# Four chunks to a cycle: a new order of score, V-product and dense matmuls in an attention and GEGLU block on one core

## The chip, the cores and the metric

The kernel runs on one core of one Trainium2 chip. The metric is the device time of one execution in microseconds: 1398.37 us, the median of 3 runs (1397.21 to 1399.72).

## The reference

A transformer block in fp32 on 2048 rows of 512: attention with 32 heads of 16 columns that share one k and one v, then a GEGLU with 1792 inner columns.

```python
h = x + A(layernorm(x), wq, wk, wv, wo)
    # q = x @ wq in 32 heads; k = x @ wk; v = x @ wv
    # softmax(q k^T * 16**-0.5) v, then @ wo
h2 = h + (gelu(xn @ w_gate) * (xn @ w_up)) @ w_down      # xn = layernorm(h)
```

## The kernel before

**Attention.** The scores are computed transposed, keys on partitions. The 2048 queries are four blocks b of 512, the 32 heads are eight groups g of four, the 2048 keys are 16 pieces kc of 128. One index i runs over all 4 x 8 x 16 = 512 of these; one i is called a *chunk* here. For a chunk, `scores` (L361 to L374) issues two *score pairs* u = 0, 1: two matmuls of 50 rows on the two halves of TensorE's array, for two heads, into a tile s of two PSUM banks, and then one exp on ScalarE (ACT) from s into half of the chunk's tile p. The tile s has two buffers (a third one in the first quarter of the run, L361 to L365), p has five (PB). `weigh` (L376 to L381) then multiplies the four heads' p with v: four matmuls on four column groups of the array, into one accumulator bank acc for the 16 chunks of a group; behind the 16th, `evacuate` copies acc to oT on VectorE (L391) and sends it by DMA to be turned and divided. Chunks that are scored and not yet weighed stand in the list `pend`; `finish(n)` weighs the n oldest.

**Dense work.** For the first three query blocks the output projection, the GEGLU's up and down products (`project`, `up`, `down`, matmul on L797) run between the attention matmuls of later blocks. Every product is split in two halves by rows of the contraction: `firsts` issues the first half (rows 0 to 63) of one product, and `seconds`, six matmuls later (LAG), the second half (rows 64 to 127) of it; the two lie side by side on the array. `step()` issues one matmul of each, and is called a *half step* here. Each half product ends in a bank of its own, out of three, that VectorE must copy or add out (L660, L664, L727) before the bank is used again; with it, `side(2)` issues up to two more VectorE operations of the GELU that are waiting in `later`. The tanh is on ACT (L676). `turn` (L623) transposes a normalized tile of h. The last block's dense work is the tail (`last_dense`, L899 and L835), after all attention.

**The order.** Nothing is scheduled by a planner: TensorE, ACT and POOL, and in this part VectorE and SP, take the order in which the code is written. After the prologue and a first quarter without dense work (`PERIOD`), a loop of `lead` scores fills the pipeline, and then the loop under L1134 runs to the end of the attention. It goes through `CYCLES`, three strings in turn: `finish(count)` at a cycle's start, then one letter a move: s a score pair, d a half step, v `finish(1)`. Three cycles take 3 + 3 + 2 chunks, 16 score pairs and 11 + 11 + 14 half steps. If there are not enough half steps available for the string (dense products wait for the normalization and the turns of a block), the cycle is *idle*: what half steps there are go first, and the second string, with single v's and no d's, is used.

Of the kernel before, what the change touches and what calls it, by code (L numbers as in the profile page):

```python
# [43 lines left out]

SETTLE = 14

CYCLES = (
    (3, "ssdddddsdddsddds", "vssvssvs"),
    (3, "ssdddddsdddsddds", "vssvssvs"),
    (2, "ssdddddsdddsdddsddds", "ssvssvss"),  # L50
)

BOUND_LISTS = (3, 4)

HOLD = -4

# [3 lines left out]
def kernel(  # L60
# [97 lines left out]
    def run(outer, first):  # L158
# [400 lines left out]
        tanhs, later = [], []  # L559
        clock = 0  # L560
# [117 lines left out]
        def gate(b, f):  # L678
            g, u, a = (halves.pop((b, f, k)) for k in range(3))

            def bring():
                nc.vector.scalar_tensor_tensor(a, a, 1.0, g, op0=ALU.add, op1=ALU.mult)

            def weigh_up():
                nc.vector.tensor_tensor(a, a, u, op=ALU.mult)

            def high():
                key = b, f // 2
                if key not in gs:
# [12 lines left out]

            return [bring, weigh_up, high, low]
# [103 lines left out]
        def step(first=True):  # L807
            nonlocal ahead, clock
            clock += 1
            if first and next(firsts, 0) is None:  # L810
                ahead += 1
            if ahead > LAG or not first:
                assert ahead > 0
                next(seconds)
                ahead -= 1
# [35 lines left out]
        last_x = []  # L851

        def prepare_x():
            b = NB - 1
            xp = sb.tile([P, TB, D], F32, tag="p", bufs=PB, name=f"xp_{b}")
            for t in range(TB):
                nc.gpsimd.dma_start(xp[:, t, :], x_t[:, b * TB + t, :])
                last_x.append(xp[:, t, :])
# [137 lines left out]
        PER = NG * KC  # L996
# [5 lines left out]
        def finish(n):  # L1002
            for _ in range(min(n, len(pend))):
                pb, pg, pkc, pp, pacc, _ = pend.pop(0)
                weigh(pacc, pp, pkc)
                if pkc == KC - 1:
                    evacuate(pb, pg, pacc)
# [9 lines left out]
        def score(n):  # L1017

            nonlocal acc
            i, u = divmod(n, 2)  # L1020
            b, r = divmod(i, PER)
            g, kc = divmod(r, KC)
            if u == 0:
                if kc == 0:
                    cur["qg"] = qgs.pop((b, g))
                    acc = psa.tile([P, T], F32, tag="acc", bufs=1, name=f"acc_{b}_{g}")
                if kc == 2 and b * NG + g + 1 < NB * NG:
                    key = divmod(b * NG + g + 1, NG)
                    qgs[key] = load_q(*key)
                cur["p"] = sb.tile([P, 4, T], F32, tag="p", bufs=PB, name=f"p_{i}")  # L1030
            scores(i, cur["p"], cur["qg"], kc, u)
            if u == 1:
                pend.append((b, g, kc, cur["p"], acc, n))
# [9 lines left out]
        width = 1  # L1043


        n, lead = 0, 2 * PER + 23
        with tc.manual_schedule(engines={mybir.EngineType.SP, mybir.EngineType.DVE}):
            parts = None
            if first:
                work = later_q()  # L1050
                parts = part_weights(early.enter_context(tc.tile_pool(name="parts", bufs=1)))


            normed = True

            def visit():
                nonlocal work, normed
                total, k = 0, None
                while work is not None and total < 6 and k != 2:
                    k = next(work, None)  # L1060
                    if k is None:
                        work = None
                        return
                    total += k
                normed = k != 4

            def norm():
                nonlocal normed
                if not normed:
                    next(work)  # L1070
                    normed = True

            def pace():
                nonlocal n, parts, db, tiny
                if n == 2 * PER:
                    drain()
                    for _ in parts or ():
                        pass
# [12 lines left out]
                if n == 2 * PER + 8:  # L1091
                    prime()

            moves = {"s": pace, "p": visit, "n": norm, "v": partial(finish, 1)}
            for move in OPENING + PERIOD * (PER // KC):
                moves[move]()
            while n < lead:
                pace()
                if n % 4 == 2 and len(pend) > 2 and n < lead - 1:
                    finish(1)  # L1100
                elif n % 4 == 0:
                    finish(len(pend) - 2)
# [5 lines left out]
        def catch_up():  # L1108
            while ahead > 0:
                step(False)  # L1110

        def before(idle):
            if outs:
                take_out()
            while (b_t := divmod(sum(turned.values()), TB)) in scaled_at:
                if clock - scaled_at[b_t] < SETTLE:
                    break
                turn(*b_t)
                if not idle:
                    break  # L1120
            bent = list(tanhs)
            tanhs.clear()
            for key in bent:
                bend(*key)
            side(100 if idle else 2)
            return bent
# [5 lines left out]
        fixed.enter_context(  # L1132
            tc.manual_schedule(engines={mybir.EngineType.SP, mybir.EngineType.DVE})
        )  # L1134
        for i in range(-((lead - end) // 16)):
            if first and i in BOUND_LISTS:
                bound_flag(BOUND_LISTS.index(i))
            for count, woven, plain in CYCLES:
                idle = available() < woven.count("d")
                if idle:  # L1140
                    while available():
                        step()
                    if at == len(queue) or queue[at][0].startswith("pg"):
                        catch_up()
                bent = before(idle)
                if n == end and not last_x:
                    prepare_x()
                if not idle:
                    finish(count)
                for key in bent:  # L1150
                    later.extend(gate(*key))
                for move in plain if idle else woven:
                    if move == "d":
                        step()
                    elif move == "v":
                        if n == end and not last_x:
                            prepare_x()
                        finish(1)
                        clock += 4
                    elif n < end:  # L1160
                        score(n)
                        n += 1
                        clock += 1
        fixed.close()
        assert not pend and not outs and at == len(queue) and left[0] == 0
        held_banks.close()
# [307 lines left out]
    def bound_flag(step):  # L1474
        if step == 0:
            nc.gpsimd.dma_start(b2, b_d)
            return
        nc.vector.tensor_reduce(b1, b2, axis=AX.X, op=ALU.max)

        nc.vector.tensor_scalar(flag, b1, (BOUND_MAX / SCALE) ** 2, None, op0=ALU.is_le)  # L1480
# [69 lines left out]
```

## Time and profile before

| | |
|---|---|
| median of 3 runs | 1398.37 us |
| the profiled execution, its own time | 1399.75 us |
| its span in the profile | 1398.0 us |
| TensorE busy | 1384.1 us, 99% |
| ACT busy | 1033.8 us, 74% |
| VectorE busy | 630.1 us, 45% |
| mean TensorE clock granted | 0.998 |

The profile names an engine's instructions by line of the kernel: PE is TensorE, PEld its weight loads, DVE VectorE. A row of the timeline has its start and its length in us, engine, line, operation, out<-in, the shape (rows x columns of the array in use, then what is read), how many like it stand in a row, and in brackets how long the engine had been idle and what ended that. A row of a group has busy time, the mean of one in ns, and the idle time before. The scores are L370, their exps L374, the V-products L378; the program's four V-products of a chunk stand in the trace as eight.

### The profile page before, as it was taken

Reading aid. Unit: us, or ns where it says so; the run is one execution under the profiler, and the core shown is the slowest. Engines: PE = TensorE matmul, PEld = TensorE weight load, DVE = VectorE, ACT = ScalarE, POOL = GpSimd, SP = SyncE. Lnnn points to the kernel's source line nnn. Section 1 sums busy time; section 2 is a strip of 40 time slices with the busy share of each in tenths; the row PEclk is TensorE's granted clock in tenths of the full one; section 3 lists DMA queues with packets and bytes.
Section 4 is the critical chain, followed back from the end, with each engine's and each line's share of the span. In section 5 each row is a group of like instructions: output and inputs, shape, how many; then the busy total and the mean of one; then the engine's idle time right before and its main releaser. Section 6 shows DMA issues by size and latency. Waiting matters only on the chain.

```text
span 1398.0 us, 25236 instructions
## 1 busy us (share of the span) xinstructions
PE 1384.1 (99%) x10430; PEld 754.1 (54%) x10430; DVE 630.1 (45%) x1013; ACT 1033.8 (74%) x1157; POOL 229.5 (16%) x334
## 2 busy tenths in 40 slices
PE   9999999999999999999999999999999999999998
PEld 7533333325555555545555555545555555558886
DVE  7413131314354444555354444446264453546665
ACT  8899999997787777877787777787778777772000
POOL 7576777721000000000000000000000000011000
PEclk9999999999999999999999999999999999999999
DMA  4466777753232332311432433320433333233552
GB/s 163 167 207 195 233 245 221 229 183 117 79 103 76 118 103 103 112 64 58 162 100 80 134 103 103 103 65 29 150 103 103 114 107 100 93 122 123 190 204 95
DMA packets 66783, 180.32 MB, mean 129 GB/s; under 512 B 9672, under 2 KB 9672, under 8 KB 66628
## 3 DMA queue, kind: packets, MB, share of 16 engines
q1 hardware_dynamic: 55324, 143.29, 31.1%
q0 software_dynamic: 10208, 35.26, 7.7%
q8 instruction: 84, 1.38, 0.4%
q14 instruction: 39, 0.32, 0.1%
q10 hardware_dynamic: 1128, 0.07, 0.1%
HBM read 130.87 MB, written 47.45 MB: 128 GB/s over the span
## 4 chain that ended last, share of the span: by engine, by line
PE 95%; ACT 2%; DVE 1%; issue 1%; DMA 1%; POOL 0%; ACTq 0%; POOLq 0%
PE acc L378 33%; PE s L370 20%; PE pu L797 9%; PE pg L797 8%; PE pd L797 7%; PE pq L219 3%; PE pd L835 3%; PE pg L835 3%; PE pu L835 3%; PE pp L797 2%; ACT p L374 2%; PE pp L899 1%; PE pd_rest L847 1%; PE pk L1295 1%; PE idle L1355 1%
## 5 line engine op out<-in xcount | busy, mean ns | idle before, releaser
L374 ACT ACTIVATE p<-s 128x1024 f32<-128x1024 f32 x1024 | 959.3, 1038 | 226.3 <-PE s L370 223.4
L378 PE MATMUL acc<-p,v_sb 128*32 128x512 f32 x4096 | 491.2, 599 | 0.0
L370 PE MATMUL s<-qg,kaug 50*128 50x512 f32 x1984 | 386.0, 427 | 4.2 <-ACT p L374 4.1
L370 PEld LDWEIGHTS s<-qg,kaug 50*128 50x128 f32 x1984 | 168.8, 184 | 282.9 <-ACT p L374 123.5
L378 PEld LDWEIGHTS acc<-p,v_sb 128*32 128x32 f32 x4096 | 108.8, 109 | 233.3 <-issue 219.9
L797 PE MATMUL pg<-x2h,w 64*128 64x512 f32 x672 | 174.8, 392 | 0.0
L797 PE MATMUL pu<-x2h,w 64*128 64x512 f32 x672 | 174.2, 392 | 0.0
L797 PE MATMUL pd<-w,gh 64*128 64x512 f32 x624 | 123.1, 394 | 0.3
L727 DVE TENSOR_TENSOR h<-h,pd 128x512 f32<-128x512 f32 x80 | 54.9, 687 | 146.0 <-PE pd L797 146.0
L137 POOL TENSOR_SCALAR rstd<-mv 128x1 f32<-128x1 f32 x16 | 3.6, 223 | 674.2 <-DVE mv L135 673.9
L797 PEld LDWEIGHTS pu<-x2h,w 64*128 64x128 f32 x672 | 95.4, 186 | 11.5
L797 PEld LDWEIGHTS pg<-x2h,w 64*128 64x128 f32 x672 | 95.1, 186 | 11.7
L797 PE MATMUL pg<-x2l,w 64*128 64x512 f32 x336 | 99.9, 392 | 0.0
L797 PE MATMUL pu<-x2l,w 64*128 64x512 f32 x336 | 99.9, 392 | 0.0
L953 ACT ACTIVATE ga<-ga 128x512 f32<-128x512 f32 x14 | 8.8, 632 | 88.5 <-DVE ga L950 88.5
L797 PEld LDWEIGHTS pd<-w,gh 64*128 64x128 f32 x624 | 67.6, 185 | 12.3 <-DVE u L664 1.4
L391 DVE COPY oT<-acc 128x512 f32<-128x512 f32 x32 | 22.1, 691 | 113.4 <-PE acc L378 113.3
L797 PE MATMUL pd<-w,gl 64*128 64x512 f32 x312 | 70.7, 391 | 0.0
L664 DVE TENSOR_TENSOR g<-g,pg 128x512 f32<-128x512 f32 x42 | 28.8, 685 | 90.6 <-PE pg L797 90.6
L414 DVE RECIPROCAL oc<-oc 128x128 f32<-128x128 f32 x64 | 56.6, 922 | 19.0 <-DMA oc<-acc_d 15.2
L660 DVE COPY g<-pg 128x512 f32<-128x512 f32 x42 | 29.1, 692 | 72.2 <-PE pg L797 72.2
L664 DVE TENSOR_TENSOR u<-u,pu 128x512 f32<-128x512 f32 x42 | 28.8, 686 | 68.7 <-PE pu L797 68.7
(252 smaller groups left out, 1468.4 us busy)
## 6 DMA issues: line engine op xcount, KB each, us to landing
w<-w_d SPq DMA_DIRECT2D x126, 512.0 KB
w<-w_d SPq DMA_DIRECT2D x21, 1024.0 KB
qg<-q_d SPq DMA_DIRECT2D x62, 200.0 KB
q_d<-qh SPq DMA_DIRECT2D x32, 256.0 KB
acc_d<-oT SPq DMA_DIRECT2D x31, 256.0 KB
oc<-acc_d SPq DMA_DIRECT2D x124, 64.0 KB
w_d<-w_0b POOLq DMA_DIRECT2D x14, 512.0 KB, 4.5
w_d<-w_1b POOLq DMA_DIRECT2D x14, 512.0 KB, 4.5
```

The source lines that it names most:

```text
L219: nc.tensor.matmul(pq, wt[c][:, d, :], xt[:, d, :], start=(n == 0), stop=(n == 3 * DC - 1),)
L370: nc.tensor.matmul(s[:, a, :], kaug[rows, kc * P : (kc + 1) * P], qg[rows, u, :], start=True, stop=True,)
L374: nc.scalar.activation(p[:, 2 * u : 2 * u + 2, :], s, AF.Exp, scale=SCALE)
L378: nc.tensor.matmul(acc[32 * j : 32 * j + 32, :], v_sb[:, kc, :], p[:, j, :], start=(kc == 0), stop=(kc == KC - 1), skip_group_check=True,)
L391: nc.vector.tensor_copy(oT, acc)
L414: nc.vector.reciprocal(oc[:, 1, sl], oc[:, 1, sl])
L660: nc.vector.tensor_copy(half, bank)
L664: nc.vector.tensor_tensor(half, half, bank, op=ALU.add)
L727: nc.vector.tensor_tensor(hs[b, t], hs[b, t], bank, op=ALU.add)
L797: nc.tensor.matmul(bank, lhsT[r], rhs[r], start=(k == 0), stop=(k == n - 1), skip_group_check=True,)
L835: nc.tensor.matmul(bank, lhsT, rhs, start=(i == 0), stop=(i == len(ts) - 1))
L847: nc.tensor.matmul(bank, lhsT, rhs, start=(i == 0), stop=(i == len(ts) - 1))
```

## The change

The three strings in turn are replaced by one, `WOVEN`, for a cycle of four chunks: `finish(4)`, then eight score pairs and twenty half steps. A cycle without enough dense work takes `SPARSE`: four times a single `finish(1)` and two score pairs, and behind every second score pair one half step if there is one (three in the first four cycles, which are always sparse). Before, an idle cycle used up its half steps at once. A cycle is sparse also if fewer than 12 half steps would be left behind it. The lead is one score longer, and its last six scores leave four chunks in `pend`, so that a cycle's four chunks lie within a group of 16. The two steps of the bound's flag stand ahead of cycles 6 and 8. The loop runs until `pend` is empty, and what half steps are left at the end follow the last V-products.

```diff
-CYCLES = (
-    (3, "ssdddddsdddsddds", "vssvssvs"),
-    (3, "ssdddddsdddsddds", "vssvssvs"),
-    (2, "ssdddddsdddsdddsddds", "ssvssvss"),
-)
-BOUND_LISTS = (3, 4)
+RUN = 4
+WOVEN = "ssdddddsdddsdddsdddsdddsddds"
+SPARSE = "vss" * RUN
+BOUND_CYCLES = (6, 8)
+OPENING_CYCLES = 4
+RESERVE = 12
...
-        n, lead = 0, 2 * PER + 23
+        n, lead = 0, 2 * PER + 24
...
-                if n % 4 == 2 and len(pend) > 2 and n < lead - 1:
+                if n > lead - 6:
+                    finish(len(pend) - RUN)
+                elif n % 4 == 2 and len(pend) > 2:
                     finish(1)
...
-            for count, woven, plain in CYCLES:
-                idle = available() < woven.count("d")
-                if idle:
-                    while available():
-                        step()
-                    if at == len(queue) or queue[at][0].startswith("pg"):
-                        catch_up()
...
+            steps = WOVEN.count("d")
+            idle = available() < steps + RESERVE or n == end or cycle <= OPENING_CYCLES
+            if idle and not available() and queue[at][0].startswith("pg"):
+                catch_up()
...
+            if not idle:
+                finish(RUN)
...
+            for move in "v" * RUN if n == end else SPARSE if idle else WOVEN:
...
+                elif n < end:
+                    score(n)
+                    n += 1
+                    clock += 1
+                    if idle and n % 2 == 0:
+                        for _ in range(3 if cycle <= OPENING_CYCLES else 1):
+                            if available():
+                                step()
+            if n == end and not pend:
+                while available():
+                    step()
```

What it does to TensorE's order is shown at three places. The names: s_i_u is the score pair u of chunk i; acc with p_i is that chunk's V-products; pg, pu and pd are dense products, with 0 or 1 ahead of the last number for the first or second half.

TensorE in the middle of the run, the V-products of chunk 296 and what stands around them, before:

```order
L370 MATMUL s_299_0_7628<-qg_2_2_6960,kaug_70 128x512 x2
L378 MATMUL acc_2_2_7324<-p_296_7547,v_sb_71 32x512 x4
L378 MATMUL acc_2_2_7324<-p_297_7568,v_sb_71 32x512 x4
L378 MATMUL acc_2_2_7324<-p_298_7603,v_sb_71 32x512 x4
L370 MATMUL s_299_1_7650<-qg_2_2_6960,kaug_70 128x512 x2
L370 MATMUL s_300_0_7655<-qg_2_2_6960,kaug_70 128x512 x2
L797 MATMUL pu_1_3_0_7624<-x2l_1_6819,w1_1_3_1_7528 128x512
```

The same place after:

```order
L374 MATMUL s_299_1_7580<-qg_2_2_6896,kaug_70 128x512 x2
L382 MATMUL acc_2_2_7268<-p_296_7488,v_sb_71 32x512 x4
L382 MATMUL acc_2_2_7268<-p_297_7508,v_sb_71 32x512 x4
L382 MATMUL acc_2_2_7268<-p_298_7535,v_sb_71 32x512 x4
L382 MATMUL acc_2_2_7268<-p_299_7563,v_sb_71 32x512 x4
L374 MATMUL s_300_0_7605<-qg_2_2_6896,kaug_70 128x512 x2
L374 MATMUL s_300_1_7609<-qg_2_2_6896,kaug_70 128x512 x2
L801 MATMUL pu_1_2_0_7548<-x2h_1_6812,w1_1_2_1_7436 128x512
```

The run of V-products has four chunks where it had three (or two), and begins and ends between whole chunks of scores.

TensorE at the end of the second block of dense work, where half steps run out, before (chunks 384 to 387 are scored):

```order
L370 MATMUL s_384_1_9895<-qg_3_0_9521,kaug_70 128x512 x2
L370 MATMUL s_385_0_9900<-qg_3_0_9521,kaug_70 128x512 x2
L378 MATMUL acc_2_7_9458<-p_382_9840,v_sb_71 32x512 x4
L370 MATMUL s_385_1_9908<-qg_3_0_9521,kaug_70 128x512 x2
L370 MATMUL s_386_0_9916<-qg_3_0_9521,kaug_70 128x512 x2
L378 MATMUL acc_2_7_9458<-p_383_9862,v_sb_71 32x512 x4
L370 MATMUL s_386_1_9931<-qg_3_0_9521,kaug_70 128x512 x2
L370 MATMUL s_387_0_9936<-qg_3_0_9521,kaug_70 128x512 x2
L378 MATMUL acc_3_0_9886<-p_384_9887,v_sb_71 32x512 x4
```

The sparse stretch at that place after (it begins at chunk 372):

```order
L382 MATMUL acc_2_7_9513<-p_372_9629,v_sb_71 32x512 x4
L374 MATMUL s_376_0_9728<-qg_2_7_9107,kaug_70 128x512 x2
L374 MATMUL s_376_1_9732<-qg_2_7_9107,kaug_70 128x512 x2
L801 MATMUL pd_1_8_1_0_9692<-w2_1_5_9122,gh_1_5_9326 128x512
L801 MATMUL pd_1_8_1_1_9716<-w2_1_4_8325,gh_1_4_8899 128x512
L382 MATMUL acc_2_7_9513<-p_373_9653,v_sb_71 32x512 x4
L374 MATMUL s_377_0_9743<-qg_2_7_9107,kaug_70 128x512 x2
L374 MATMUL s_377_1_9747<-qg_2_7_9107,kaug_70 128x512 x2
L801 MATMUL pd_1_8_1_0_9692<-w2_1_5_9122,gl_1_5_9327 128x512
L801 MATMUL pd_1_8_1_1_9716<-w2_1_4_8325,gl_1_4_8900 128x512
```

Single chunks of V-products stood there in five places in a row before; now there are twenty, chunks 372 to 391, with one half step behind each two score pairs.

TensorE at the end of the attention, before:

```order
L370 MATMUL s_511_1_13249<-qg_3_7_12468,kaug_70 128x512 x2
L797 MATMUL pd_2_11_1_0_13233<-w2_2_6_12533,gl_2_6_13060 128x512
L797 MATMUL pd_2_11_0_1_13226<-w2_2_6_12533,gl_2_6_13060 128x512
L797 MATMUL pd_2_11_1_0_13233<-w2_2_6_12533,gh_2_6_13059 128x512
L797 MATMUL pd_2_11_1_1_13258<-w2_2_5_12531,gh_2_5_12768 128x512
```

And after:

```order
L374 MATMUL s_511_1_13198<-qg_3_7_12430,kaug_70 128x512 x2
L801 MATMUL pd_2_8_1_0_13129<-w2_2_5_12562,gh_2_5_12876 128x512
L801 MATMUL pd_2_8_1_1_13203<-w2_2_4_11763,gh_2_4_12312 128x512
L382 MATMUL acc_3_7_12820<-p_508_13145,v_sb_71 32x512 x4
L382 MATMUL acc_3_7_12820<-p_509_13160,v_sb_71 32x512 x4
L382 MATMUL acc_3_7_12820<-p_510_13175,v_sb_71 32x512 x4
L382 MATMUL acc_3_7_12820<-p_511_13193,v_sb_71 32x512 x4
L801 MATMUL pd_2_8_1_0_13129<-w2_2_5_12562,gh_2_5_12876 128x512
```

Before, ten beats of dense matmuls and then two chunks of V-products follow the last score; after, one half step, four chunks of V-products and then the rest of the dense products, 26 beats.

More of the change, by code (lines that the diff above doesn't have):

```diff
@@ L1134, in run @@
         )
-        for i in range(-((lead - end) // 16)):
-            if first and i in BOUND_LISTS:
-                bound_flag(BOUND_LISTS.index(i))
-            for count, woven, plain in CYCLES:
-                idle = available() < woven.count("d")
-                if idle:
-                    while available():
-                        step()
-                    if at == len(queue) or queue[at][0].startswith("pg"):
-                        catch_up()
[L1145 to L1163, printed above, removed]
+        cycle = 0
@@ new lines, in run @@
+        while pend:
+            if first and cycle in BOUND_CYCLES:
+                bound_flag(BOUND_CYCLES.index(cycle))
+            cycle += 1
+            steps = WOVEN.count("d")
+            idle = available() < steps + RESERVE or n == end or cycle <= OPENING_CYCLES
+            if idle and not available() and queue[at][0].startswith("pg"):
+                catch_up()
+            bent = before(idle)
+            if n == end and not last_x:
+                prepare_x()
+            if not idle:
+                finish(RUN)
+            for key in bent:
+                later.extend(gate(*key))
+            for move in "v" * RUN if n == end else SPARSE if idle else WOVEN:
+                if move == "d":
+                    step()
+                elif move == "v":
+                    finish(1)
+                    clock += 4
+                elif n < end:
[8 more added lines that the diff above has]
+                while available():
+                    step()
```

## Prediction

> **What bounds the kernel now.** I read the page first, then TensorE's timeline in the middle of the run, then the stretches in which TensorE has no dense work. In the words of the code: a *chunk* is one index i, that is two score pairs (two 50-row matmuls each), two exps on ACT and one chunk of V-products (eight matmul records on L378, four instructions in the program). A *half step* is one beat of the dense products: a 64-row matmul of one product beside one of another, on the two halves of the array.
>
> ```profile
> span 1398.0 us, 25236 instructions
> ...
> PE 1384.1 (99%) x10430; PEld 754.1 (54%) x10430; DVE 630.1 (45%) x1013; ACT 1033.8 (74%) x1157; POOL 229.5 (16%) x334
> ...
> PE 95%; ACT 2%; DVE 1%; issue 1%; DMA 1%; POOL 0%; ACTq 0%; POOLq 0%
> ...
> L374 ACT ACTIVATE p<-s 128x1024 f32<-128x1024 f32 x1024 | 959.3, 1038 | 226.3 <-PE s L370 223.4
> ```
>
> The chain is TensorE for 95% of the span. Busy 99% says little, since ends are modelled; what counts is the distance from one start to the next. Here is one woven stretch, of TensorE alone:
>
> ```profile
> 702.74 2.78 PE L378 MATMUL acc<-p,v_sb 128*32 128x512 f32 x24
> ...
> 719.45 0.40 PE L797 MATMUL pu<-x2l,w 64*128 64x512 f32 x1
> ...
> 720.61 0.40 PE L370 MATMUL s<-qg,kaug 50*128 50x512 f32 x2
> 720.85 0.39 PE L797 MATMUL pu<-x2h,w 64*128 64x512 f32 x2
> ...
> 721.53 0.40 PE L370 MATMUL s<-qg,kaug 50*128 50x512 f32 x2
> ...
> 722.47 0.40 PE L370 MATMUL s<-qg,kaug 50*128 50x512 f32 x2
> 722.80 2.78 PE L378 MATMUL acc<-p,v_sb 128*32 128x512 f32 x24
> 725.51 0.73 PE L370 MATMUL s<-qg,kaug 50*128 50x512 f32 x4
> 726.08 0.39 PE L797 MATMUL pg<-x2h,w 64*128 64x512 f32 x1
> ...
> 728.22 0.39 PE L370 MATMUL s<-qg,kaug 50*128 50x512 f32 x2
> 728.45 0.63 PE L797 MATMUL pg<-x2h,w 64*128 64x512 f32 x4
> ...
> 729.49 1.92 PE L378 MATMUL acc<-p,v_sb 128*32 128x512 f32 x16
> 731.34 0.74 PE L370 MATMUL s<-qg,kaug 50*128 50x512 f32 x4
> ```
>
> From the starts: five half steps take 1.16 us (719.45 to 720.61), three take 0.68, so 0.233 each; a score pair takes 0.235 (728.22 to 728.45), but 0.33 with a run of V-products behind it (722.47 to 722.80); the two pairs behind a run take 0.57 (725.51 to 726.08), 0.10 more than two. A run of three chunks takes 2.71 and a run of two 1.85: 0.86 a chunk and 0.14 once. So every run of V-products, however long, costs 0.10 + 0.14 + 0.10 = **0.34 us** beside its chunks. A round of three old cycles (8 chunks, 36 half steps, 3 runs) takes 20.06 (702.74 to 722.80). A run that comes straight after half steps pays the same 0.10:
>
> ```profile
> 1251.57 0.40 PE L797 MATMUL pd<-w,gl 64*128 64x512 f32 x2
> ...
> 1253.99 1.92 PE L378 MATMUL acc<-p,v_sb 128*32 128x512 f32 x16
> 1255.84 0.50 PE L899 MATMUL pp<-wo_hi,o_hi 128*128 128x512 f32 x1
> ```
>
> In the order this stretch is four paired and six single half steps: 10 x 0.232 + 0.10 = 2.42. The run ends at 1255.84, where the tail begins.
>
> **The change part by part.**
>
> *Woven cycles.* A new cycle has 4 chunks, 20 half steps and one run, so two of them are an old round with four more half steps and one run fewer: (20.06 + 4 x 0.233 - 0.34) / 2 = 10.32 us. The order has 75 of them: 774.0 us. The old rounds would take 300 x 20.06 / 8 + 150 x 0.233 = 787.2 for that work. **Gain 13.2 us.** ACT must not become the bound in them: a score pair now comes every 0.235 + 0.70 = 0.935 us five times in a row, on two score buffers.
>
> ```profile
> 719.42 4.69 ACT L374 ACTIVATE p<-s 128x1024 f32<-128x1024 f32 x5 [1.47 <-PE s L370]
> ```
>
> Five exps take 4.69, the last about 1.02 long (row of 942.05, below): 0.92 from start to start, just under 0.935; cost taken as nothing, and ACT then rests in the longer run of 3.57 (4 x 0.86 + 0.14), which also covers the tanh that stands behind a cycle's exps.
>
> *Sparse cycles.* The half steps that woven cycles now use up faster are missing later. In the order 48 chunks become "one run of one chunk, two pairs, one half step". TensorE alone: 1.00 (run of one, 938.41 to 939.40) + 0.57 + 0.23 + 0.10 = 1.90. The old kernel's stretch without dense work shows what else holds there:
>
> ```profile
> 933.62 0.91 PE L370 MATMUL s<-qg,kaug 50*128 50x512 f32 x4
> ...
> 935.45 0.50 PE L370 MATMUL s<-qg,kaug 50*128 50x512 f32 x2
> 936.15 0.49 PE L370 MATMUL s<-qg,kaug 50*128 50x512 f32 x2 [0.20 <-ACT p L374]
> 936.58 1.06 PE L378 MATMUL acc<-p,v_sb 128*32 128x512 f32 x8
> 937.57 0.91 PE L370 MATMUL s<-qg,kaug 50*128 50x512 f32 x4
> 938.41 1.06 PE L378 MATMUL acc<-p,v_sb 128*32 128x512 f32 x8
> 939.40 0.49 PE L370 MATMUL s<-qg,kaug 50*128 50x512 f32 x2
> ```
> ```profile
> 934.16 3.77 ACT L374 ACTIVATE p<-s 128x1024 f32<-128x1024 f32 x4 [0.19 <-PE s L370]
> ...
> 942.05 1.02 ACT L374 ACTIVATE p<-s 128x1024 f32<-128x1024 f32 x1 [0.17 <-PE s L370]
> ```
>
> The score at 933.62 starts its exp at 934.16 (0.54 later), the second exp follows 0.92 later and lasts 1.02, and only then (2.48, plus 0.05) may the second pair of the next chunk use that buffer: at 936.15, which is 2.53 after 933.62. So two chunks take 3.95 (933.62 to 937.57). With the half step, the next chunk's second pair would come at 1.90 + 0.34 = 2.24, before 2.53: it waits 0.29, and a pair that has waited takes up to 0.10 longer (0.43 from 936.15 to 936.58, not 0.33; before a half step I take 0.07, between that and nothing). The chunk behind it, 2.27 later, finds its buffers free. So chunks take 1.90 and 2.27 in turn, **2.08** in the mean, 48 x 2.08 = 99.8 us. An old woven chunk costs (20.06 - 36 x 0.233) / 8 = 1.46 without its half steps, so old rounds would do 48 chunks and 48 half steps in 81.2. **Loss 18.6 us**, nearly all of it 0.34 for each single run and the ACT wait.
>
> *The opening.* The lead is one score longer, and ACT still sets its pace there, so the run of V-products behind it comes one exp later: 311.09 + 0.92 + 0.33 = 312.34 (old: 311.52):
>
> ```profile
> 311.09 0.51 PE L370 MATMUL s<-qg,kaug 50*128 50x512 f32 x2 [0.41 <-ACT p L374]
> 311.52 2.78 PE L378 MATMUL acc<-p,v_sb 128*32 128x512 f32 x24
> ```
> ```profile
> 962.01 0.66 PE L623 MATMUL pxt<-ident,xb 128*128 128x128 f32 x4
> 962.59 0.64 PE L378 MATMUL acc<-p,v_sb 128*32 128x512 f32 x4
> ```
>
> From there to the first run of four (chunk 160) the order has: run of two, pairs and lone half steps, 3.4 with a wait of 0.2; 15 chunks with three half steps, 1.00 + 0.57 + 0.70 + 0.10 = 2.37 each, 35.5; three turns of a tile at 0.58 less the 0.10, 1.4; six lone half steps that let the second half catch up, 1.4; eight chunks of about 2.09 (one with a turn), 16.7. Sum 58.5.
>
> *The end.* The last run of four, 3.57, then 26 half steps alone, 6.1 + 0.10: 9.7 together. The old kernel went from its last run straight to the tail. The tail's own order is unchanged. The old tail began with 39 matmuls in 9.07 us, 0.233 each, so nothing waited there for the last copy-out, and 6 us more of cover buy nothing:
>
> ```profile
> 1255.91 9.07 PE pp L899 x39
> ```
> ```profile
> 1247.58 2.24 POOL L857 DMA_DIRECT2D xp<-in_A_x_dram  x4 [270.58 <-ACT p L374]
> ```
>
> *At nothing:* the flag's two steps (DMA and VectorE) stand two cycles apart, 20 us, as before (closer, VectorE would stand until the DMA lands); loads of q and of weights are issued at the same chunk and the same product end, so SP's queue keeps its order; prepare_x (L857, 2.24 us of issue on POOL) stands ahead of the last run, with that run and 26 half steps as cover; bare, it would cost at least those 2.24.
>
> *The sum.* From 312.34: 58.5 + 774.0 + 99.8 + 8 turns x 0.58 (4.6) + 9.7 = 946.6. To that 2 us for waits at turns and for banks, as here, where products of nine half steps end too close for VectorE:
>
> ```profile
> 915.23 0.40 PE L797 MATMUL pd<-w,gl 64*128 64x512 f32 x2
> 915.76 0.50 PE L797 MATMUL pd<-w,gh 64*128 64x512 f32 x2
> ```
>
> 0.53 where 0.23 is usual. (Bounds: 0 if they fall into sparse chunks, 5 if 12 turns and some 10 such products wait 0.2 each.) The tail would begin at 312.34 + 948.6 = 1260.9, against 1255.84: **5.1 us later**. The count of runs says why the idea yields so little: from there on 149 old runs (91 of three, 45 of two, 13 single) become 148 (76 of four, one of two, 71 single). The profiled span of 1398.0 becomes 1403.1; that execution took 1399.75, 1.4 above the median of 1398.37, and on the median I forecast **1403.5 us**.
>
> **The rivals.** 0.2% (2.8 us) is about what a measurement of this kernel can tell from no change.
>
> *Faster: the half step pays for itself in sparse chunks.* If ACT were early enough, say because an exp's 0.54 of delay shrinks when ACT has a backlog, the 48 chunks would take 1.90: 8.6 us less, 3.5 us under the old time, 1394.9. It decides where the second pair of a sparse chunk shows no wait. Against it: the row at 936.15, whose cause (two buffers, 2.53 us) is still there. Chance 0.09.
>
> *No change.* The sparse wait halves (-4), or turns and banks wait nothing (-2), or both: 1397 to 1401. For it: the balance is a small difference of 13 gained and 18 lost. Chance 0.16.
>
> *Slower still: VectorE cannot clear banks in twenty half steps.* Each finished half product costs it 0.69 and brings up to two more such operations:
>
> ```profile
> L414 DVE RECIPROCAL oc<-oc 128x128 f32<-128x128 f32 x64 | 56.6, 922 | 19.0 <-DMA oc<-acc_d 15.2
> L660 DVE COPY g<-pg 128x512 f32<-128x512 f32 x42 | 29.1, 692 | 72.2 <-PE pg L797 72.2
> ```
>
> That is 2.07 for every six half steps with two pairs, 1.87 us. It falls behind 0.2 each time, three times a cycle, and has 1.1 in hand (1.87 less its copy); with two reciprocals (1.84) queued at a cycle's start it may just fail. At 0.1 us in each of 75 cycles 7 us more: 1411. Chance 0.08, within "slower".
>
> *ACT paces the woven cycles.* If an exp there took its group's mean of 1.038 us instead of 0.92, five pairs in a row would each come 0.10 late: 0.5 x 75 = 38 us, 1441. The row of five in 4.69 speaks against it. Chance 0.03. [...]
>
> **How the numbers follow.** The forecast's own case (3 to 10 us slower) has 0.64; with the two slower rivals slower by over 0.2% has 0.75, within 0.2% 0.16, faster 0.09. The range runs from the upper part of "no change", 1398.5, to 1410: the forecast with both unknowns at their high end (3 us for turns and banks, and 0.05 us a cycle on VectorE, 3.5 us).
>
> **What would show it.** Right: runs of four every 10.3 us; runs of one in sparse stretches at 1.9 and 2.3 us in turn, with "ACT p L374" named before every second pair; the first run of four near 371 us; the tail's first L899 matmul near 1261. Wrong: sparse chunks all at 1.90 (faster); woven cycles of 10.5 or more with VectorE or ACT named before a half step or a score (slower still); or another number of runs than counted.

## The result, and the profile after

The changed kernel takes **1421.46 us** (median of 4 runs, 1420.83 to 1422.14) against 1397.88 for the kernel before in the same comparison (4 runs, 1397.21 to 1399.72): ratio **1.0165** [1.0153, 1.0177], slower by 23.6 us. The forecast was 1403.5, with a range up to 1410. So the direction was right and the size more than four times too small: the forecast's difference on the profiled span was 5.1 us, the measured one is 21.1 (1419.1 against 1398.0). The 16 us between them are what the rest of this text is about.

From the page of the profile after, the span and the chain of waits by engine:

```profile
span 1419.1 us, 25238 instructions
...
PE 88%; ACT 7%; DVE 2%; DMA 1%; issue 1%; POOL 1%; SPq 0%; ACTq 0%; POOLq 0%; DVEq 0%
```

TensorE's share of the chain falls from 95% to 88%, and ACT's rises from 2% to 7%. TensorE's waits between the opening and the tail (us in total, how many, the longest), before (311 to 1256) and after (311 to 1277):

```profile
PE s L370 <- ACT p L374: 2.3, 8, 0.4
PE pxt L623 <- DMA oc<-acc_d: 0.3, 1, 0.3
```
```profile
PE s L374 <- ACT p L378: 6.6, 30, 0.4
PE pxt L627 <- DVE x2l L633: 3.6, 2, 2.0
PE pu L801 <- DMA w<-w_d: 1.8, 2, 1.2
PE pxt L627 <- DVE h L614: 1.2, 2, 0.6
```

A woven cycle after, the scores (L374) and V-products (L382) of TensorE's timeline:

```profile
393.57 3.64 PE L382 MATMUL acc<-p,v_sb 128*32 128x512 f32 x32
...
397.14 0.74 PE L374 MATMUL s<-qg,kaug 50*128 50x512 f32 x4
...
398.87 0.46 PE L374 MATMUL s<-qg,kaug 50*128 50x512 f32 x2
...
403.96 2.35 PE L382 MATMUL acc<-p,v_sb 128*32 128x512 f32 x20
```
```profile
397.75 7.44 ACT L378 ACTIVATE p<-s 128x1024 f32<-128x1024 f32 x8 [2.42 <-PE s L374]
```

From run to run it is 10.39 us (393.57 to 403.96), not 10.32. The row at 398.87 is the third pair: its matmuls last 0.46 instead of the usual 0.40. It takes the buffer of the first pair, whose exp is only just done (397.75 + 1.02 = 398.77); in the mean of the cycles the step behind the third pair comes 0.304 later instead of the 0.238 of e1 below. The first exp starts 0.61 behind its pair (397.75 after 397.14), not 0.54, and eight exps then take 7.44, that is about 0.92 from one to the next, as forecast. In the program's order the first exp of a chunk waits for two semaphores (its scores, and ACT's own earlier work on the buffer p), the second exp for its scores alone. Before, two cycles in three began with a chunk's second pair; the change puts a first pair behind every run of V-products. In the third, here from 705.45, the old kernel shows the same late exp (0.60) and the same slow third pair:

```profile
705.45 0.73 PE L370 MATMUL s<-qg,kaug 50*128 50x512 f32 x4
...
707.17 0.46 PE L370 MATMUL s<-qg,kaug 50*128 50x512 f32 x2
```
```profile
706.05 4.69 ACT L374 ACTIVATE p<-s 128x1024 f32<-128x1024 f32 x5 [1.53 <-PE s L370]
```

A sparse stretch after, of TensorE:

```profile
924.54 1.07 PE L382 MATMUL acc<-p,v_sb 128*32 128x512 f32 x8
...
926.24 0.49 PE L374 MATMUL s<-qg,kaug 50*128 50x512 f32 x2 [0.20 <-ACT p L378]
...
926.89 1.06 PE L382 MATMUL acc<-p,v_sb 128*32 128x512 f32 x8
927.89 0.75 PE L374 MATMUL s<-qg,kaug 50*128 50x512 f32 x4
...
928.79 0.64 PE L382 MATMUL acc<-p,v_sb 128*32 128x512 f32 x4
```

The two lengths in turn are there, with ACT named at every other second pair: 2.35 (924.54 to 926.89) and 1.90 (926.89 to 928.79), mean 2.125, where 2.27 and 1.90 had been forecast.

The opening, first V-products behind the lead, and the clock in the six microseconds ahead of it and the six from there (the columns after the stretch are its length, the busy time of PE, PEld, DVE, ACT and POOL, and PEclk):

```profile
312.33 2.86 PE L382 MATMUL acc<-p,v_sb 128*32 128x512 f32 x16
315.12 1.22 PE L374 MATMUL s<-qg,kaug 50*128 50x512 f32 x4
```
```profile
306.00:312.00 6.00, 4.34 (x28) 1.55 (x24) 3.02 (x5) 6.00 (x8) 0.00 (x0) 1.00 0.97 345
312.00:318.00 6.00, 6.00 (x33) 2.11 (x33) 0.00 (x0) 4.53 (x5) 0.00 (x0) 0.72 1.00 393
```

The run begins at 312.33, 0.01 from the forecast. But a run of two chunks then takes 2.79 (312.33 to 315.12), where 1.85 is usual: TensorE's granted clock is at half for 3.4 us (0.72 in the mean of six).

The turns and the weights. The two turns of one idle cycle, and a half step that waits for its weights:

```profile
670.73 0.66 PE L627 MATMUL pxt<-ident,xb 128*128 128x128 f32 x4
672.99 0.63 PE L627 MATMUL pxt<-ident,xb 128*128 128x128 f32 x4 [1.60 <-DVE x2l L633]
```
```profile
710.97 0.46 PE L801 MATMUL pu<-x2h,w 64*128 64x512 f32 x1 [1.20 <-DMA w<-w_d]
```
```profile
693.27 1.45 SPq L548 DMA_DIRECT2D w<-w_d  x3
697.14 0.33 SPq L447 DMA_DIRECT2D acc_d<-oT  x1
705.02 2.11 SPq L413 DMA_DIRECT2D oc<-acc_d  x4
707.23 0.37 SPq L537 DMA_DIRECT2D w<-w_d  x1
```

Two turns in a row share one bank, so the second waits until VectorE has taken the first out of it (1.60); TensorE stands there with nothing else in its order. The last fence is SP's queue: three loads of w2 (1 MB each), the write of a group's accumulator, then the reads of it, which are issued at 705.02, 7.9 us behind the write, and only then the load of w1 that the half step at 710.97 needs. Before, the write stood 17 us behind the loads of w2, and the reads came 2.0 us behind it:

```profile
674.87 1.44 SPq L544 DMA_DIRECT2D w<-w_d  x3
...
692.05 0.32 SPq L443 DMA_DIRECT2D acc_d<-oT  x1
694.09 1.72 SPq L409 DMA_DIRECT2D oc<-acc_d  x4
```

The end: the tail begins 16 us behind the 1260.9 of the forecast.

```profile
1276.88 0.50 PE L903 MATMUL pp<-wo_hi,o_hi 128*128 128x512 f32 x1
```

### The profile page after: what moved, and what is told of

The parts are those of the page before. It is cut to its first block, busy times and chain, and to the rows that moved or that the text cites. A ratio compares the mean times of both kernels' runs of the same rounds, so it can differ in the third digit from the quotient of the medians.

```text
span 1419.1 us, 25238 instructions
## 1 busy us (share of the span) xinstructions
PE 1393.7 (98%) x10430; PEld 754.9 (53%) x10430; DVE 632.3 (45%) x1013; ACT 1032.8 (73%) x1157; POOL 228.9 (16%) x334
## 4 chain that ended last, share of the span: by engine, by line
PE 88%; ACT 7%; DVE 2%; DMA 1%; issue 1%; POOL 1%; SPq 0%; ACTq 0%; POOLq 0%; DVEq 0%
PE acc L382 31%; PE s L374 19%; PE pg L801 8%; PE pu L801 8%; PE pd L801 6%; ACT p L378 6%; PE pq L223 3%; PE pd L839 3%; PE pg L839 3%; PE pu L839 3%; PE pp L801 2%; DMA w<-w_d 1%; PE pp L903 1%; PE pd_rest L851 1%; PE pxt L627 0%
## 5 line engine op out<-in xcount | busy, mean ns | idle before, releaser
L382 PE MATMUL acc<-p,v_sb 128*32 128x512 f32 x4096 | 491.6, 600 | 0.0
L374 PE MATMUL s<-qg,kaug 50*128 50x512 f32 x1984 | 393.3, 432 | 9.2 <-ACT p L378 9.2
L374 PEld LDWEIGHTS s<-qg,kaug 50*128 50x128 f32 x1984 | 173.9, 184 | 290.1 <-ACT p L378 180.6
L382 PEld LDWEIGHTS acc<-p,v_sb 128*32 128x32 f32 x4096 | 108.4, 109 | 241.8 <-issue 240.8
L801 PEld LDWEIGHTS pg<-x2l,w 64*128 64x128 f32 x336 | 47.5, 186 | 5.9
```

The source lines that it names most:

```text
L374: nc.tensor.matmul(s[:, a, :], kaug[rows, kc * P : (kc + 1) * P], qg[rows, u, :], start=True, stop=True,)
L382: nc.tensor.matmul(acc[32 * j : 32 * j + 32, :], v_sb[:, kc, :], p[:, j, :], start=(kc == 0), stop=(kc == KC - 1), skip_group_check=True,)
L801: nc.tensor.matmul(bank, lhsT[r], rhs[r], start=(k == 0), stop=(k == n - 1), skip_group_check=True,)
```

## The experiments

Each kernel is the changed one with the edit shown, unless another is named. Single runs stand beside one run of the kernel before on the same chip: 1398.82 (e1 to e4), 1396.45 (e5 to e8); for e9 to e11 the median before is 1397.9. Two kernels, e10 and e12, were timed in rounds.

**e1: the lead one score longer**, so that a woven cycle begins with the second pair of a chunk, and a sparse chunk's half step stands between two pairs.

```diff
-        n, lead = 0, 2 * PER + 24
+        n, lead = 0, 2 * PER + 25
```

> Edit: the lead is one score longer, so that the pair behind every run of V-products is a chunk's second pair, not its first; in sparse chunks the half step then falls between the two pairs. Theory A (a chunk's first exp waits for one thing more, the p tile, and starts 0.60 instead of 0.54 us after its scores): woven cycles go from 10.39 to 10.32-10.33 us, the third pair of a cycle waits 0 instead of 0.07, 75 x 0.065 = 5 us less from that alone; sparse chunks fall below 2.05. Rival B (the 0.07 comes from ACT having rested longer, about 3 us, in the longer run of V-products): woven cycles stay at 10.39. In both the half step between the pairs takes some 0.1 us from each sparse chunk. Total by A 1408 to 1413, by B 1414 to 1417.

Measured: 1409.63 us. The same places, ACT and TensorE:

```profile
394.36 7.44 ACT L378 ACTIVATE p<-s 128x1024 f32<-128x1024 f32 x8 [2.38 <-PE s L374]
```
```profile
393.82 0.73 PE L374 MATMUL s<-qg,kaug 50*128 50x512 f32 x4
...
395.54 0.40 PE L374 MATMUL s<-qg,kaug 50*128 50x512 f32 x2
```

The first exp is back at 0.54 behind its pair, the third pair no longer waits (0.40, where it was 0.46), an undisturbed cycle is 10.31 in the mean, and sparse chunks take 1.98. That is 11 of the 23.6 us for one number: about 6 from the sparse chunks, 3 ahead of the first run of four, and 5.7 from woven cycles, of which a longer wait for weights, with half clock behind it, takes 3.5 back. Of the 3 us, 1.4 are chance: they stand ahead of 292 us, where the two orders are the same, and there the profile of the change has a stretch of half clock (from 285.88) that this one lacks. The half clock of the opening is absent here too. That alignment costs the 0.07 is shown; that the second semaphore is why is read from the order, and no run took it away by itself.

**e2: only the half step of a sparse chunk moved between its two pairs.**

```diff
-                    if idle and n % 2 == 0:
+                    if idle and n % 2 == 1:
```

> Edit: in sparse chunks the half step stands between the two score pairs instead of behind them; nothing else. Theory A (the second pair waits for the exp two before it, 2.60 us after the first pair before): the wait of 0.36 in every second chunk shrinks by the 0.23 of the half step, chunks take 1.90 and about 2.1 in turn, mean 2.0 instead of 2.125: 48 x 0.12 = 6 us less, 1415. Rival B (the sparse chunks are bound by ACT's own throughput): 2.125 stays, 1421. Woven cycles 10.39 by both.

Measured: 1414.40 us, sparse chunks 2.01 in the mean (2.125), woven cycles still 10.39. The half step that stood behind a late second pair now stands where TensorE waits for ACT anyway.

**e3: V-products among the last scores of the lead**, so that TensorE has more to do there.

```diff
+                elif n > lead - 14:
+                    finish(len(pend) - 3)
```

> Edit: the four waiting chunks are built up in three steps over the last 14 scores of the lead, not in one gap of six scores without V-products. Theory A (in that gap TensorE does so little that its clock is halved for 3.4 us at 313): no half-clock stretch near 313, the run behind the lead takes 1.86 instead of 2.79, 1.4 to 2 us less, 1419 to 1420. Rival B (the half clock comes at this place from the change of PSUM pools or whatever the order): it stays, 1421.5.

Measured: 1418.99 us. The same six microseconds:

```profile
312.00:318.00 6.00, 6.00 (x42) 2.15 (x34) 0.00 (x0) 5.17 (x6) 0.00 (x0) 1.00 1.03 418
```

The clock stays at 1.00 and 42 matmuls run where 33 did; from the first V-products to the first run of four it is 59.1 us rather than 60.5, so the half clock was worth 1.4. That the edit keeps it away is not shown. In e4, whose lead is that of the change, it is absent as well, and the opening takes 59.1 too:

```profile
312.00:318.00 6.00, 5.92 (x40) 2.47 (x40) 0.77 (x2) 5.16 (x7) 0.00 (x0) 1.00 1.02 409
```

**e4: one turn at a time, behind V-products.**

```diff
+        def turn_one():
+            b_t = divmod(sum(turned.values()), TB)
+            if b_t in scaled_at and clock - scaled_at[b_t] >= SETTLE:
+                turn(*b_t)
...
-            while (b_t := divmod(sum(turned.values()), TB)) in scaled_at:
-                if clock - scaled_at[b_t] < SETTLE:
-                    break
-                turn(*b_t)
-                if not idle:
-                    break
+            turn_one()
...
+            if not idle:
+                finish(RUN)
             bent = before(idle)
...
-            if not idle:
-                finish(RUN)
...
+            for at_move, move in enumerate(moves):
+                if idle and at_move == 6:
+                    turn_one()
```

> Edit: a woven cycle's run of V-products stands ahead of the turn of a tile (L627) instead of behind it, and a sparse cycle makes two turns apart instead of one behind the other. Theory A (a turn waits for a PSUM bank that VectorE is still emptying, 0.7 us when it stands behind half steps, and 1.6 to 2 us for the second of two turns): the stretches around chunks 264 to 276 and 396 to 408 lose 5 to 7 us, 1414 to 1417. Rival B (what waits is the normalized tile or the products behind the turns): the wait moves on to the next products and the time stays within 2 us of 1421.

Measured: 1418.54 us, between the two theories. Cycle by cycle against the change: the cycles of chunks 264, 272, 396 and 400 are 1.2 to 1.7 shorter, 5.9 together, and the turns now stand in other cycles for 1.5; the opening, without half clock, is 1.4 shorter; but the cycle of chunk 288 grows from 11.81 to 14.91, since a wait there is 2.8 rather than 1.2 and half clock (from 710.12) follows it. So theory A holds for the turns (4.4 us net), and the cycle of chunk 288 gave 3.1 of it back. TensorE's waits from 311 to 1290 show no turn any more. The longest single one is this, with what VectorE does at its end:

```profile
PE pu L801 <- DVE u L668: 2.8, 1, 2.8
```
```profile
706.92 1.76 DVE L418 RECIPROCAL oc<-oc 128x128 f32<-128x128 f32 x2 [7.47 <-DMA oc<-acc_d]
708.61 0.63 DVE L668 TENSOR_TENSOR u<-u,pu 128x512 f32<-128x512 f32 x1
```

The weights had landed 1.1 us before it ended; what ended it is VectorE, which takes its work in order and stood 7.47 us at the late reads of the accumulator. So those reads cost time in two ways: through the loads that queue behind them, and through VectorE.

**e5: the reads of the accumulator issued by POOL.**

```diff
-                    nc.sync.dma_start(oc[r0 : r0 + DH, :, :], view[j])
+                    nc.gpsimd.dma_start(oc[r0 : r0 + DH, :, :], view[j])
```

> The changed kernel, with the four reads of the turned accumulators (oc<-acc_d, L413) issued by POOL instead of SP. Theory A: the two stalls for weights (cycles of chunk 288 and of chunk 420, 11.8 and 11.2 us where 10.4 is usual) come from SP's queue: those reads stand in it, wait for the write of acc_d, which stands behind the loads of w2, and the next load of w1 waits behind them. Then both stalls go, those cycles take about 10.5, and the kernel takes 2 us less, about 1419. Theory B: the weights are late because the DMA engines are full of the w2 loads; then the stalls stay and the time is 1421 as before.

Measured: 1445.09 us. The cycle of chunk 288 falls to 10.40 and that of chunk 420 stays long, 11.42, but the edit costs some 25 us elsewhere. In the first quarter POOL splits weights and cannot issue the reads in time; VectorE stands at its next operation on them, the copy of the accumulator queues behind that, and TensorE waits for the accumulator's bank. VectorE's wait (in the stretch from 260 to 285) and TensorE's:

```profile
DVE oc L418 <- DMA oc<-acc_d: 9.6, 1, 9.6
```
```profile
278.71 1.94 PE L382 MATMUL acc<-p,v_sb 128*32 128x512 f32 x8 [6.95 <-DVE oT L395]
```

In this wait and behind it the clock is at half (273.67 to 283.91). Theory A holds for chunk 288, not for chunk 420, and the sum was wrong, because I had looked only at the queue that the reads leave and not at the one that they enter.

**e6: e1 with sparse runs of two chunks.**

```diff
-SPARSE = "vss" * RUN
+SPARSE = "vvssss" * (RUN // 2)
```

> The kernel of e1_shift (1409.63), with sparse cycles of two runs of two chunks, four score pairs and two half steps each, in place of four single runs: the same chunks and half steps in about 31 runs fewer. Theory A: a sparse chunk is paced by its exps, 0.92 each on two score buffers, and a longer run only makes ACT rest longer: two chunks then take about 2.43 + 0.33 + 1.86 = 4.6 to 4.7 (2.33 a chunk, 1.99 in e1_shift), in the opening 0.1 a chunk less; the kernel takes about 14 us more, 1420 to 1427. Theory B, the account of the prediction taken by runs alone (0.34 us each): 31 runs fewer, 10 us less, 1399.

Measured: 1442.16 us, 32.5 more than e1. The sparse stretch:

```profile
942.08 1.92 PE L382 MATMUL acc<-p,v_sb 128*32 128x512 f32 x16
...
945.55 0.51 PE L374 MATMUL s<-qg,kaug 50*128 50x512 f32 x2 [0.65 <-ACT p L378]
...
946.46 0.50 PE L374 MATMUL s<-qg,kaug 50*128 50x512 f32 x2 [0.17 <-ACT p L378]
946.89 1.92 PE L382 MATMUL acc<-p,v_sb 128*32 128x512 f32 x16
```

Two chunks take 4.81 (942.08 to 946.89), with 0.82 of waiting for ACT, against 3.96 in e1. Fewer runs, and slower: in the sparse stretches exps set the pace, and counting 0.34 a run (theory B) has the wrong sign. My 14 us were too few: 4.81 for 4.6 to 4.7, half clock in the opening, and 2 us more for weights.

**e7: e1, e4 and e5 together.** The edits are those shown.

> The edits of e1_shift, e4_late and e5_queue together. Theory A: the added cost of the change is the sum of separate waits, so their removal adds up: 1421 less 11.3 (e1_shift), less about 4.4 (turns in e4_late), less 2 (weights), less up to 3 for the two stretches at half clock that the stalls set off in e1_shift: 1399.5 to 1403, within 0.3% of the kernel before, with woven cycles of 10.33 and sparse chunks of 1.99. Theory B: the waits hide one another (a wait that goes uncovers the next one on ACT or for a bank): 1406 or more.

Measured: 1424.12 us. Inconclusive for its question: against e1 the turns' cycles are 5.0 shorter, as expected, but reads on POOL bring 10.6 in the first quarter and 3.0 and 4.0 in the cycles of chunks 268 and 352. The cycle of chunk 288, 10.40 in e5, takes 13.87 here: TensorE waits 3.30 for VectorE, which stands 8.01 at a read that POOL issues late. e10 repeats it without POOL.

**e8: e7 with eighteen half steps a cycle.**

```diff
-WOVEN = "ssdddddsdddsdddsdddsdddsddds"
+WOVEN = "ssdddddsdddsddsdddsddsddds"
```

> The kernel of e7_together with eighteen half steps in a woven cycle instead of twenty: 84 woven cycles and 12 sparse chunks behind the opening, where there were 75 and 48. Theory A: ACT, 0.92 an exp on two score buffers, then sets the length of a woven cycle: its eighth pair comes 6.1 us behind the first, and with 0.33 and the run of 3.57 the cycle takes 10.03; 84 x 10.03 + 12 x 1.99 = 866.4 against 75 x 10.33 + 48 x 1.99 = 870.3: 4 us less than e7_together. Theory B: TensorE alone counts, 10.33 - 2 x 0.233 = 9.87 a cycle: 17 us less than e7_together.

Measured: 1469.05 us; waits set off by the reads on POOL (one of 11.5) spoil the time, but undisturbed cycles answer the question:

```profile
784.53 3.64 PE L382 MATMUL acc<-p,v_sb 128*32 128x512 f32 x32
...
793.38 0.49 PE L374 MATMUL s<-qg,kaug 50*128 50x512 f32 x2
...
794.75 1.49 PE L382 MATMUL acc<-p,v_sb 128*32 128x512 f32 x12
```
```profile
788.64 7.44 ACT L378 ACTIVATE p<-s 128x1024 f32<-128x1024 f32 x8 [2.26 <-PE s L374]
```

A cycle is 10.22 (784.53 to 794.75): two half steps fewer save 0.10 of their 0.47. The seventh pair (793.38) comes when the fifth exp is done: 788.64 + 4 x 0.92 + 1.02 = 793.34, so ACT paces it. My 10.03 had left out that the exp waited for counts with its whole 1.02, and that a pair that waits takes 0.10 longer. At 84 cycles of 10.22 and 12 sparse chunks of 1.98, 882 us against the 870 of the expectation, fewer half steps would lose.

**e9: the reads two cycles later, still by SP.**

```diff
-                if b == 0 and g < NG - 1:
-                    outs.append([turn_out])
+                if g < NG - 1:
+                    outs.extend([[turn_out]] if b == 0 else [[], [turn_out]])
```

> The changed kernel, with the four reads of the turned accumulators (oc<-acc_d, L413) issued two cycles behind the write that they wait for, still by SP, so that the next loads of w1 stand ahead of them. Theory A (SP's queue holds the weights back): the cycle of chunk 288 goes from 11.8 to 10.4 us, as it did in e5_queue, and nothing else is added; the cycle of chunk 420, which e5_queue left at 11.2, keeps its wait; 1419 to 1420. Theory B (the DMA engines are full of w2): chunk 288 stays at 11.8 and the time at 1421.

Measured: 1421.14 us. The cycle of chunk 288 falls to 10.36, as theory A has it; but the cycle of chunk 420 goes from 11.20 to 14.46, with 2.3 of waiting for w1 (the same load issued ahead of the reads, right behind 3 MB of w2) and half clock behind it (from 1047.30). So there are two causes: at chunk 288 SP's queue, at chunk 420 a load that is issued only just behind those of w2; the second is argued from the order of issue, no run moved the w2 loads.

**e10: e1, e4 and e9 together.**

> The edits of e1_shift, e4_late and e9_defer together (e7_together with the reads on SP, late, instead of on POOL). Theory A, the added cost is a sum of separate waits: 1409.6 (e1_shift) less 4.5 for the turns (as e7_together shows against e1_shift in the cycles of chunks 264 to 280 and 396 to 406) less 4.7 for the cycle of chunk 288 (15.04 in e1_shift, where a stretch at half clock is part of it): 1400.4, between 1399.5 and 1402.5, which is 0.1 to 0.3% over the kernel before. Theory B, a wait that goes uncovers another: 1405 or more.

Measured: **1405.62 us** (1404.43 to 1408.0), ratio to before 1.0054 [1.0036, 1.0072]. The turns' cycles are 5.8 shorter than in e1 (1.5 of it a stretch of half clock that stood there in e1), as theory A has it. Chunk 288 is 11.76 rather than 15.04 (forecast 10.35): a wait of 1.2 for weights is left, which e9 alone did not have, and no run settles why. And the profiled execution, the longest, has the half clock again in its opening, 2.9 us. No wait of a new kind shows.

**e11: e1 with the old bursts**: a sparse cycle behind the first four does all half steps at hand ahead of it.

```diff
-            if idle and not available() and queue[at][0].startswith("pg"):
+            if idle and cycle > OPENING_CYCLES:
+                while available():
+                    step()
+            if idle and not available() and (at == len(queue) or queue[at][0].startswith("pg")):
                 catch_up()
```

> The kernel of e1_shift, but a sparse cycle behind the first four does all half steps at hand in one burst ahead of it, as the old idle cycles did: some 5 woven cycles become 20 sparse chunks, and about 100 half steps go into bursts. Theory A: a sparse chunk is paced by its exps (1.98) with or without a half step, so a half step in it is nearly free and one in a burst costs 0.233: 20 x 1.98 + 100 x 0.233 - 5 x 10.33 = 11 us more than e1_shift, 1417 to 1425. Theory B: TensorE pays 0.233 for a half step wherever it stands, and a sparse chunk without one takes 1.75: 1409 to 1413.

Measured: 1435.49 us, 26 more than e1. A sparse stretch without half steps, and the wait of the bursts:

```profile
612.39 1.07 PE L382 MATMUL acc<-p,v_sb 128*32 128x512 f32 x8
...
616.35 1.06 PE L382 MATMUL acc<-p,v_sb 128*32 128x512 f32 x8
```
```profile
PE pd L801 <- DVE gh L698: 7.7, 3, 2.6
```

Two chunks take 3.96 (612.39 to 616.35), exactly as with half steps in e1: there a half step is free. My 11 us had too few half steps in the bursts: by the order about 130, net of those that stood at the end, 30 us instead of 23. With that, 20 x 1.98 + 30 - 5 x 10.33 = 18, and the 7.7 of waiting for VectorE (a burst asks for the GELU of the last columns at once) makes 26. That it fits so well is in part luck: the sum leaves out the half clock behind each of the three waits, and that the cycle of chunk 288 is 10.30 here, not the 15.04 of e1.

**e12: e10 with the edit of e3.**

> The kernel of e10_three with the edit of e3_lead (three chunks stay pending in the last fourteen scores of the lead, so that V-products stand between the scores there). Theory A, the half clock in the opening is the last separate term that can be taken out: e10_three took 1404.4 to 1408.0, the longest in the profiled execution, which shows half clock from 310.7 to 316.5; here it should show none, and the kernel take 1402.5 to 1405, where the forecast's own sum (1403.5) lies. Theory B, the half clock only moves to another place, or costs nothing: 1405 to 1408 again.

Measured: **1404.45 us** (1402.64 to 1405.46), ratio 1.0045 [1.0028, 1.0062]. The clock in the opening:

```profile
312.00:318.00 6.00, 6.00 (x40) 2.28 (x40) 0.00 (x0) 5.68 (x7) 0.00 (x0) 1.00 1.01 399
```

There is no half clock in this one profile; the profiled execution's span is 1402.7. That the edit of e3 is worth something on top of e10 is not shown: 1404.43 to 1408.0 there and 1402.64 to 1405.46 here overlap. The tail begins at 1258.62, 2.3 us ahead of the forecast's 1260.9, and is 1.9 longer than that of before. Of this, 1.6 lie behind VectorE's last operation, where only the last write and the program's end are left (7.17 us, 5.60 before; e5 and e10 show 7.49 and 7.34 there); why is open.

## Why the prediction was wrong, point by point

- **The count of runs, the 75 woven cycles, the 48 sparse chunks, the start at 312.34, ACT's 0.92 an exp** came out as written, the start with some luck: the profiles before and after both have a stretch of half clock at 286 us, and e2 and e9, with the same lead and none there, start at 311.1. The idea that a gain in woven cycles is paid back in sparse chunks is right. That e12 lies at 1404.45 beside the forecast's 1403.5 is in part luck too: its sparse chunks (1.97, not 2.08) save 5.1 us and its earlier start 1.4, while its turns and waits take 4.0 more than the sum has for them, and its tail 1.9.
- **Woven cycles: 10.38 in the mean of the 66 undisturbed ones instead of 10.32**, 4.7 us in 75. The step "cost taken as nothing" for ACT failed: the sum used a row of five exps that began with a chunk's second pair, and the change moved a first pair there. e1 gives 10.31.
- **Sparse chunks: 2.125 instead of 2.08**, 2.1 us in 48: the same 0.07, now in the wait behind the first exp. e1 and e2 remove more than that (1.98 and 2.01), since the half step stood in the wrong gap.
- **Opening: 60.5 instead of 58.5.** The clock was not in the sum at all: it is 59.1 in e3 and e4, without the half clock, so 1.4 of the 2.0. With e1's alignment it is 58.7 (e1, e12).
- **Waits at turns, banks and for weights: 8.7 instead of 2** beside the turns' own 4.6, the largest miss, and above even the bound of 5 that stood beside it. The step that weights are issued "at the same product end, so SP's queue keeps its order" failed: the order stayed, but the groups' ends, and with them the write and the reads of the accumulator, now fall on the loads of w2; and two turns in one idle cycle had no V-products between them. e4 shows the turns. For the weights, e5 and e9 show the queue as the cause at chunk 288; at chunk 420 the cause is argued.
- **The end: 10.1 instead of 9.7.**

Together 4.7 + 2.1 + 2.0 + 6.7 + 0.4 = 15.9 of the 16 us. Of the rivals, VectorE's banks in woven cycles and ACT's pace at 1.04 were both absent (half steps 0.70 for three throughout, exps 0.92). The high end of the range allowed 3 us for turns and banks and 0.05 a cycle on VectorE, but each term's error had the same sign. In a kernel whose TensorE waits only 2.6 us in 945, a new order has almost no wait to remove and many places to add one.

## What to carry to other kernels

When an order of work is realigned, take each duration from rows that stand in the new alignment, or give the term a bound for it: 0.07 us, paid once a cycle behind a first exp, came to some 5 us in 75 cycles. Price what the old order kept apart without saying so, such as two turns, or a load and a write on one queue, and not only what the new order joins. Where one engine paces a stretch, as ACT does the sparse chunks, work on another is free there, and fewer, longer runs on the other can make it slower.

## What the runs showed of the hardware

- TensorE's clock fell to half for 3.4 us in the opening, without any long idle gap, behind six scores that ACT paces: TensorE was 4.34 us busy in the six ahead of it. The Trainium skill (TensorE: Matmul & The Clock Gate, Part 1: The HAM clock gate) describes a free-running activity window of 3413 ns and a half-rate state; the stretch here agrees, 3.413 us at half rate.
- The stretches show such a window: within one execution their starts lie on one grid of 3.413 us. In the changed kernel 285.88 and 313.18 are 8 lengths apart, in e1 666.76 and 707.72 are 12, in e9 671.83 and 1047.30 are 110.
- So it is partly chance what falls into one window. In the changed kernel the window from 309.77 to 313.18 held 2.28 us of TensorE's work, and half clock followed; in e4, with the same order there, the same place fell into two windows (307.35 to 310.76 to 314.17) with 2.57 and 2.59, and none followed. In e1 half clock followed a wait of 2.9 for weights, and the cycle of chunk 288 took 15.04, against 11.81 where the wait was 1.2; in e7 a wait of 3.30 (716.73 to 720.03) lay across the grid's line at 718.29, and none followed.
- How much work is too little isn't settled. In e1 the opening's window held 2.30 us and none followed, and neither did it behind a window with 1.56 (991.03 to 994.44).
- The first exp behind a pause of ACT started 0.61 behind its scores in one alignment and 0.54 in the other.
